# GpSimd makes the last shifted copy of a key tile as one addition of 32-bit integers

## The chip, the cores and the metric

The kernel runs on one core of a Trainium2 chip. The core has TensorE for matrix products (PE, with PEld for loading its weights), VectorE (DVE), ScalarE (ACT), GpSimd (POOL) and SyncE (SP), which issues most transfers. PE writes only to PSUM; the other tiles lie in SBUF. The metric is the device time of one execution in microseconds; less is better. A profile is taken of one execution, and its span is the time from its first to its last instruction.

## The reference

A token matrix x (2048 x 512) goes through two blocks whose results are mixed by a gate for each token:

```python
x = A_x
g = _sigmoid((x * gate_w).sum(-1, keepdims=True))
a = _A_ref(x, A_wqkv, A_wo)                         # attention
b = _B_ref(x, B_w_gate, B_w_up, B_w_down)           # (silu(x @ w_gate) * (x @ w_up)) @ w_down
return g * a + (1 - g) * b

def _A_ref(x, wqkv, wo):
    ...                                             # q, k, v: 32 heads of width 16
    scores = jnp.einsum("bhqd,bhkd->bhqk", q, k) * (Dh ** -0.5)
    p = _softmax(scores, axis=-1)
    o = jnp.einsum("bhqk,bhkd->bhqd", p, v)
    return ... @ wo
```

The attention needs 32 x 2048 x 2048 exponentials. They are the large elementwise work of the kernel.

## The kernel before, in words

**Units and tiles.** The 32 heads are handled in 8 groups of 4, the 2048 queries in 4 blocks of 512. One block of queries with one group of heads is a unit; there are 32. A unit has 16 key tiles of 128 keys. One key tile of a unit is 4 heads x 128 keys x 512 queries: four matmuls of scores, each 128 x 512 in one bank of PSUM, and after the exponential one product with the values ("term") of four small matmuls that run side by side in PE and add into o_ps (function pv, line 972).

**Two ways to the exponential.** Most key tiles go to ACT: PE writes scores to s_t (two tiles of two banks each), ACT turns 128 x 1024 at a time into e_all, PE multiplies it with vaug: one term. Other tiles go to DVE (emit_d, line 845). There PE writes the scores of one head to d_t, in one of three single banks that the feed-forward block uses too (m_tile, line 361), and DVE evicts it with a multiplication and an addition into 16-bit integers, y, whose bits read as bf16 are a rough exponential (line 862). Four evictions of 128 x 512 fill one tile y of 128 x 2048. This rough exponential is bettered in one of two ways:
- *two terms* (groups[n] == 2, lines 869 to 871): DVE takes two parts of y's bits by masks into two more buffers (bits, line 895), multiplies one by y (product, line 904), and PE multiplies both results with the values;
- *four terms* (lines 872 to 876): y itself and three copies of it, each with a constant of SHIFTS (25, 56, 94) added to the 16-bit integers (copy, line 887), so that four rough exponentials with errors at different places are summed by PE.

**Buffers.** y and the copies lie in seven homes of 128 x 2048 16-bit values (NS = 7; six of their own, named c_t, and one that lies in wd_t early on and in kaug's first group later; home, line 836). A home is free when all its users are through: users[i] holds a count and the latest time, and drop (line 823) counts down. y is counted twice for a four-term tile, once for its own term and once for its copies. At most NY = 3 tiles y are alive (y_live).

**The order is written out by a planner.** As the program is built, a plan keeps a clock for PE, DVE and ACT (plan.pe, plan.dve, plan.act), with a price for each instruction, and the functions at the end of the kernel choose at each step which instruction comes next. Engines take their instructions in the order in which they were recorded (ordered, line 156), so the choice is fixed at build time; on the chip only semaphores hold an engine back.
- The main loop (line 1563) issues the scores for ACT at the latest 0.64 us (LATEST) before the plan's ACT runs out of work, and fills PE's time before that with terms whose data the plan holds to be ready (pv_list, line 1403; the list vready has the time from which a term of DVE may be used) and with pieces of the projections and of the feed-forward block.
- fill_dve (line 924) chooses what DVE does next: copies and masks (vops), evictions of d_t (d_wait) or other evictions and elementwise work (owed).
- v_unit (line 1517) says whether another key tile can go to DVE: the last tile of the unit that is worked on, or of the next, if the plan's DVE is through with what it has LEAD (8.0 us, in the last unit LAST, 6.0) before ACT would be through with the unit. v_take then takes the tile away from ACT, and quad (line 1542) says whether it is made with two terms or with four: four where PE had time to spare (spare[0]).

So the counts of tiles on ACT and on DVE, of two-term and four-term tiles, and the order on every engine come out of the plan, and they change when a price in it changes. POOL only clears tiles at the start.

Of the kernel before, what the change touches and what calls it, by code (L numbers as in the profile page):

```python
# [9 lines left out]
ALU = mybir.AluOpType  # L10
AX = mybir.AxisListType
BF16 = mybir.dt.bfloat16
F32 = mybir.dt.float32
U16 = mybir.dt.uint16
F16 = mybir.dt.float16


# [62 lines left out]
def kernel(  # L80
# [12 lines left out]
    nc = tc.nc  # L93
    P = 128
# [10 lines left out]
    QBW = 512  # L105
# [15 lines left out]
    NV = 4  # L121
# [6 lines left out]
    SHIFTS = (25.0, 56.0, 94.0)  # L128
# [12 lines left out]
    const = ctx.enter_context(tc.tile_pool(name="const", bufs=1))  # L141
# [38 lines left out]
            return lambda *a, **kw: ordered(f(*a, **kw))  # L180

    vec = Ordered(nc.vector)
    queue = Ordered(nc.sync)


# [95 lines left out]
    for j in range(4):  # L281
        nc.gpsimd.memset(sel_t[32 * j:32 * j + 1, j:j + 1], 1.0)

    kb = const.tile([P, NB], F32, name="kb")
    gval = const.tile([P, KT], F32, name="gval")
    omg = const.tile([P, KT], F32, name="omg")
# [4 lines left out]


    class Plan:
        pe = dve = act = 0.0
        mode = last = None
        seq = 0
        slot = -1
# [2 lines left out]
    plan = Plan()  # L300
# [10 lines left out]
    FLIP, UNIT_US = 0.105, 0.217  # L311
    TO_ACT, ACT_FIX, ACT_COL, ACT_IN = 0.485, 0.064, 0.4265, 0.167
    ACT_PE, DVE_PE, PE_DVE, ACT_DVE = 0.055, 0.08, 0.24, 0.06

    def spend(mode, mms, ready=0.0):

        plan.seq += 1
        work_at.append((plan.pe, mms))
        plan.pe = max(plan.pe + (FLIP if mode != plan.mode else 0.0), ready) + (0.226 if mode == "F" else UNIT_US) * mms
        plan.mode = mode  # L320
# [40 lines left out]
    def m_tile(name):  # L361
        while m_ready() is None:
            stuck()
        i = min((i for i in range(NM) if banks[i] is not None), key=lambda i: banks[i])
        plan.pe = max(plan.pe, banks[i])
        banks[i] = None
        held[i] = ps_m[i].tile([P, QBW], F32, tag=f"m{i}", name=name)
        return held[i]

    def m_free(ps, t):  # L370
        i = [h is ps for h in held].index(True)
        banks[i], held[i] = t + DVE_PE, None
# [159 lines left out]
    def q_pieces(qb, b):  # L532
# [11 lines left out]
        def end(p, me):  # L544
# [7 lines left out]
            def mag():  # L552
                vec.tensor_scalar(out=aq[:, :].bitcast(U16), in0=qst[:, :].bitcast(U16), scalar1=0x8000, scalar2=None,
                                  op0=ALU.bitwise_or)
                plan.chain = me
                later(0.21, weigh, plan.dve, ("q", b))
# [9 lines left out]
    def q0_pieces(qb):  # L566
# [11 lines left out]
        def clear():  # L578
            vec.tensor_scalar(out=mt[:, 5, :].bitcast(U16), in0=mt[:, 5, :].bitcast(U16), scalar1=0x7FFF, scalar2=None,
                              op0=ALU.bitwise_and)  # L580
# [108 lines left out]
    vops = []  # L689
    c_free = [0.0] * NS  # L690
# [3 lines left out]
    vready = []  # L694
# [4 lines left out]
    def score(ps, b, rows=64):  # L699
        n, j = b // 4, HEADS[b % 4]  # L700
        (qb, g), kt = UNIT[n // KT], n % KT
        r = slice(32 * j // rows * rows, 32 * j // rows * rows + rows)
        q = (q0a if n < KT // 2 else q0[qb])[r, j % 2, :] if g == 0 else get_q(qb, g)[r, j % 2, :]
        mm(ps, lhsT=kaug[r, g, kt * P:(kt + 1) * P], rhs=q, start=True, stop=True,
           tile_position=(r.start, 0))
# [115 lines left out]
    users = {}  # L821

    def drop(i, t):
        u = users[i]
        u[:] = u[0] - 1, max(u[1], t)
        if not u[0]:
            c_free[i] = u[1]

    def take_home():
        i = min(range(NS), key=lambda i: c_free[i])  # L830
        t, c_free[i] = c_free[i], 1e9
        assert t < 1e9
        users[i] = [1, 0.0]
        return i, t

    def home(i=None, t=0.0):

        if i is None:
            i, t = take_home()
        plan.dve = max(plan.dve, t)  # L840
        if i < NS - 1:
            return i, vex.tile([P, NV * QBW], U16, tag=f"h{i}", name="c_t", bufs=1)[:, :]
        return i, (kaug[:, 0, :] if au > QB else wd_t[:, 0:4, :].rearrange("p f d -> p (f d)")).bitcast(U16)

    def emit_d(i, rows=32):
        if not vcur:
            n = v_take()
            waiting[n] = [NV, None, take_home()]
            vcur.update(n=n, left=list(range(NV)), y=None)
            y_live[0] += 1  # L850
        n, left, cur = vcur["n"], vcur["left"], waiting[vcur["n"]]
        left.remove(i)
        d_t = m_tile("d_t")
        score(d_t[:, :], 4 * n + i, rows)
        if not left:
            vcur.clear()

        def first():
            if cur[1] is None:
                cur[1] = home(*cur[2])  # L860
            h, y = cur[1]
            vec.tensor_scalar(out=y[:, i * QBW:(i + 1) * QBW], in0=d_t[:, :], scalar1=EXP_A, scalar2=EXP_B[groups[n]],
                              op0=ALU.mult, op1=ALU.add)
            m_free(d_t, plan.dve)
            cur[0] -= 1
            if cur[0]:
                return
            plan.last = ("y", n)
            if groups[n] == 2:
                vops.extend([(0.6, lambda: bits(n, 0, y), ("y", n), n, True), (0.6, lambda: bits(n, 1, y), None, n, True),  # L870
                             (MUL_US, lambda: product(n, h, y), None, n, False)])
            else:
                users[h][0] = 2
                ready(n, 0, h, y)
                for k in range(1, 4):
                    vops.append((0.6, lambda k=k: copy(n, k, h, y), ("y", n) if k == 1 else None, n, True))
        d_wait.append((plan.pe + UNIT_US + PE_DVE, first, n))

    waiting = {}
    copies = {}  # L880
    part = {}

    def ready(n, k, h, c):
        copies[n, k] = (c.bitcast(BF16), h)
        vready.append((plan.dve + DVE_PE, n, k))

    def copy(n, k, i, y):
        h, c = home()
        vec.tensor_scalar(out=c, in0=y, scalar1=SHIFTS[k - 1], scalar2=None, op0=ALU.add)
        ready(n, k, h, c)  # L890
        if k == 3:
            drop(i, plan.dve + 0.05)
            y_live[0] -= 1

    def bits(n, k, y):
        h, c = home()
        if k == 0:
            vec.tensor_scalar(out=c, in0=y, scalar1=0x007F, scalar2=0x3F00, op0=ALU.bitwise_and, op1=ALU.bitwise_or)
            part[n] = (h, c)
        else:  # L900
            vec.tensor_scalar(out=c, in0=y, scalar1=0xFF80, scalar2=None, op0=ALU.bitwise_and)
            ready(n, 0, h, c)

    def product(n, h, y):
        i, c = part.pop(n)
        vec.tensor_tensor(out=c.bitcast(BF16), in0=y.bitcast(BF16), in1=c.bitcast(BF16), op=ALU.mult)
        ready(n, 1, i, c)
        drop(h, plan.dve + 0.05)
        y_live[0] -= 1
# [411 lines left out]
    for pos, qb in enumerate(ORDER):  # L1321
# [13 lines left out]
        for tq in range(TQ):  # L1335

            def cond(qb=qb):
                return qb == QB - 1 or all((qb, b) in normed for b in range(NB))
            rel = 100 if pos == 0 else (UNIT.index((qb, G - 1)) + 1) * KT + 16
            c = pace.add((out_pieces if pos else down_pieces)(qb, tq), rel, a0 + per * (0.64 + 0.36 * (tq + 1) / TQ),  # L1340
                         (gus if tq == 0 else prev) + gates, cond=cond)
# [10 lines left out]
    au = at_ = quarter = begun = 0  # L1352
    vu = 0
    hi = [KT] * UNITS
# [151 lines left out]

    SLACK = 0.04
    CUTS = 4
    LEAD, LAST = 8.0, 6.0
    TILE_US = 1.82  # L1510

    def forward():
# [4 lines left out]
    def v_unit():  # L1517

        nonlocal vu
        if y_live[0] >= NY or min(c_free) >= 1e9 or sum(v[0] for v in vops) > 4.9 or (au, at_) < (0, 2):  # L1520
            return None
        while vu < UNITS:
            if vu > au + 1 or vu in q_of and not (q_of[vu].done() and (vu < QB or plan.slot >= q_of[vu].done_at + 3)):
                return None
            left = hi[vu] - (at_ + begun if vu == au else 0)
            if vu >= au and left > 0 and (vu or hi[0] > KT // 2):
                end = plan.act + (left - 1) * TILE_US + ((hi[au] - at_) * TILE_US if vu > au else 0.0)
                busy = sum(v[0] for v in vops) + 0.6 * (len(owed) + len(d_wait))
                if plan.dve + busy + (LEAD if vu < UNITS - 1 else LAST) <= end:
                    return vu  # L1530
            vu += 1
        return None

    def v_take():
        un = v_unit()
        hi[un] -= 1
        n = un * KT + hi[un]
        groups[n] = 2 if quad() else 4
        forward()
        return n  # L1540
# [7 lines left out]
    def wants():  # L1548

        if len(d_wait) >= 3 or not vcur and v_unit() is None:  # L1550
            return 0
        return 2 if thirst() < 1.5 else 1
# [10 lines left out]
    while au < UNITS:  # L1563
# [11 lines left out]
        if room > 0.02:  # L1575
# [3 lines left out]
            c = side(room + SLACK)  # L1579
# [30 lines left out]
    while closed < UNITS or vops or vcur:  # L1610
# [9 lines left out]
        c = side(2.0)  # L1620
# [38 lines left out]
    for tq in range(TQ):  # L1659
        t = (QB - 1) * TQ + tq  # L1660
# [39 lines left out]
```

## Time and profile before

| | us |
|---|---|
| time, median of 3 runs | 769.66 (769.5 to 769.75) |
| the profiled execution's own time | 768.54 |
| its span | 766.8 |
| ACT busy in it | 750.8 |
| PE busy | 740.6 |
| DVE busy | 734.6 |
| POOL busy | 10.6 |

The span leaves out what lies around the first and the last instruction: 768.54 - 766.8 = 1.7 us. The granted TensorE clock is 0.999 of full speed. In the rows of the profile, L171 is the helper that records every ACT instruction, L168 that of PE and L180 that of DVE, so groups are told apart by the names of their tiles: e_all<-s_t is an exponential, c_t<-d_t an eviction of scores into y, TENSOR_SCALAR c_t<-c_t of 128x2048 a shifted copy or a mask, TENSOR_TENSOR c_t<-c_t the product of a two-term tile. A row has the count, then the busy time of all and the mean of one in ns, then the idle time of the engine just before them and what ended it. Instructions of one engine overlap a little, so means times counts are more than the busy time.

### The profile page before, as it was taken

What the parts mean: (1) busy time and instruction counts of PE and PEld (TensorE: products, weight loads), DVE (VectorE), ACT (ScalarE), POOL (GpSimd) and SP (SyncE); (2) the same over time, 40 slices, a digit from 0 to 9 for tenths busy, and PEclk for the clock granted to TensorE, in tenths of its full rate; (3) what the DMA queues carried; (4) which work ended last, traced back from release to release, by engine and by line L of the source; (5) the groups of instructions that cost most, each with busy time, mean ns of one, the idle gap of its engine ahead of it and who ended that gap; (6) DMA issues with size and microseconds to landing.
All of it is one profiled execution on the core that took longest, in us unless ns stands there. A gap on an engine that the chain in (4) does not pass through costs nothing.

```text
span 766.8 us, 24169 instructions
## 1 busy us (share of the span) xinstructions
PE 740.6 (97%) x10109; PEld 246.0 (32%) x10109; DVE 734.6 (96%) x1234; ACT 750.8 (98%) x843; POOL 10.6 (1%) x25
## 2 busy tenths in 40 slices
PE   8999999999999999999999999999999999999997
PEld 3333333333333233333333333323333333333332
DVE  7899999999999999999999999999999999999993
ACT  6999999999999999999999999999999999999996
POOL 5000000000000000000000000000000000000000
PEclk9999999999999999999999999999999999999999
DMA  9000313144210013211200130212000232100001
GB/s 222 6 2 15 67 21 78 34 117 87 62 28 13 17 41 78 58 33 28 51 18 24 32 95 21 69 28 56 12 19 17 69 80 56 31 18 7 22 30 35
DMA packets 91029, 34.53 MB, mean 45 GB/s; under 512 B 75488, under 2 KB 90472, under 8 KB 90920
## 3 DMA queue, kind: packets, MB, share of 16 engines
q1 hardware_dynamic: 89192, 32.66, 17.7%
q8 instruction: 79, 1.29, 0.7%
q10 hardware_dynamic: 1728, 0.33, 0.2%
q14 instruction: 30, 0.25, 0.1%
HBM read 21.55 MB, written 2.35 MB: 31 GB/s over the span
## 4 chain that ended last, share of the span: by engine, by line
ACT 48%; PE 27%; DVE 13%; issue 11%; DMA 0%; DVEq 0%; ACTq 0%
ACT e_all L171 45%; DVE c_t L180 9%; PE s_t L168 9%; PE o_ps L168 8%; PE gu L168 5%; ACT th L171 2%; PE dps L168 2%; DVE kaug L180 1%; PE qp L168 1%; DVE mt L180 1%; PE vp L168 1%; PE warm L168 1%; DVE gs L180 1%; DVE osb L180 1%; PE kp L168 0%
## 5 line engine op out<-in xcount | busy, mean ns | idle before, releaser
L171 ACT ACTIVATE e_all<-s_t 128x1024 bf16<-128x1024 f32 x774 | 722.9, 1049 | 3.2 <-PE s_t L168 1.6
L180 DVE TENSOR_SCALAR c_t<-d_t 128x512 uint16<-128x512 f32 x432 | 285.8, 681 | 4.8 <-PE d_t L168 4.5
L168 PE MATMUL s_t<-qx,kaug 32*128 32x512 bf16 (+1 forms) x1224 | 237.6, 385 | 11.6 <-ACT e_all L171 10.2
L168 PE MATMUL o_ps<-e_all,vaug 128*32 128x512 bf16 (+3 forms) x2024 | 170.1, 334 | 0.8 <-ACT e_all L171 0.6
L168 PEld LDWEIGHTS <-kaug 32*128 32x128 bf16 (+1 forms) x2048 | 80.6, 91 | 275.8 <-issue 268.6
L180 DVE TENSOR_SCALAR c_t<-c_t 128x2048 uint16<-128x2048 uint16 x236 | 157.7, 682 | 0.4
L168 PE MATMUL d_t<-qx,kaug 32*128 32x512 bf16 x408 | 153.2, 384 | 0.3 <-DVE qx L180 0.3
L168 PEld LDWEIGHTS <-vaug 128*32 128x32 bf16 x4112 | 101.9, 95 | 131.8 <-issue 94.7
L168 PE MATMUL o_ps<-c_t,vaug 128*32 128x512 bf16 (+3 forms) x1768 | 136.3, 341 | 0.7 <-DVE osb L180 0.6
L168 PE MATMUL gu<-xT,wg 128*32 128x512 bf16 x896 | 71.9, 383 | 0.1
L168 PE MATMUL gu<-xT,wu 128*32 128x512 bf16 x896 | 70.2, 383 | 0.0
L168 PE MATMUL ops<-wd_t,mt 128*32 128x512 bf16 x672 | 58.1, 382 | 0.0
L180 DVE TENSOR_SCALAR kaug<-d_t 128x512 uint16<-128x512 f32 x60 | 40.0, 682 | 0.9 <-PE d_t L168 0.7
L180 DVE SCALAR_TENSOR_TENSOR mt<-gs,gu 128x512 bf16<-128x512 bf16 x56 | 38.1, 680 | 1.6
L180 DVE TENSOR_TENSOR c_t<-c_t 128x2048 bf16<-128x2048 bf16 x32 | 38.8, 1214 | 0.0
L168 PE MATMUL s_t<-q,kaug 32*128 32x512 bf16 (+1 forms) x188 | 36.4, 385 | 2.4 <-ACT e_all L171 2.2
L180 DVE SCALAR_TENSOR_TENSOR gs<-th,gu 128x512 bf16<-128x512 bf16 x56 | 38.0, 678 | 0.1
L171 ACT ACTIVATE th<-gu 128x512 bf16<-128x512 f32 x56 | 35.0, 624 | 0.0
L168 PEld LDWEIGHTS <-mt 128*32 128x32 bf16 (+1 forms) x1037 | 25.0, 95 | 26.2 <-issue 19.6
L180 DVE TENSOR_SCALAR kaug<-c_t 128x2048 uint16<-128x2048 uint16 x46 | 31.3, 680 | 0.0
L180 DVE TENSOR_SCALAR c_t<-kaug 128x2048 uint16<-128x2048 uint16 x42 | 28.1, 683 | 0.0
L168 PEld LDWEIGHTS <-wg 128*32 128x32 bf16 x896 | 18.1, 94 | 25.3 <-issue 21.3
(142 smaller groups left out, 434.1 us busy)
## 6 DMA issues: line engine op xcount, KB each, us to landing
wg<-in_B_w_gate_dram SPq DMA_DIRECT2D x56, 128.0 KB
wu<-in_B_w_up_dram SPq DMA_DIRECT2D x56, 128.0 KB
on<-osb SPq DMA_DIRECT2D x120, 16.0 KB
rb<-rr SPq DMA_DIRECT2D x15, 128.0 KB
wd_t<-in_B_w_down_dram SPq DMA_DIRECT2D x7, 256.0 KB
qx<-qst SPq DMA_DIRECT2D x96, 16.0 KB
qx<-aq SPq DMA_DIRECT2D x96, 16.0 KB
out_dram<-o_t SPq DMA_DIRECT2D x12, 128.0 KB
```

Of the source, the lines that this page charges most:

```text
L168: return ordered(nc.tensor.matmul(*args, **kw))
L171: ordered(nc.scalar.activation(*args, **kw))
L180: return lambda *a, **kw: ordered(f(*a, **kw))
```

## The change

For a four-term tile the third copy (shift 94) is given to POOL when a home is free and POOL's clock in the plan is less than 4 us ahead of DVE's. POOL reads y as 1024 integers of 32 bits for each partition and adds lift, a tile with 94 in both 16-bit halves, broadcast along the row. The addition is recorded when the last eviction of the tile is, so it waits for that eviction and for its home. The plan books 2.5 us for it; y then has three users, and the copies that are left for DVE are two. Where it is not given, DVE makes three copies as before.

```diff
+    gps = Ordered(nc.gpsimd)
...
+    lift = const.tile([P, 2], U16, name="lift")
+    nc.gpsimd.memset(lift[:], int(SHIFTS[2]))
...
-        pe = dve = act = 0.0
+        pe = dve = act = pool = 0.0
...
+    POOL_US, POOL_PE, POOL_AHEAD = 2.5, 0.15, 4.0
...
             else:
-                users[h][0] = 2
+                gives = min(c_free) < 1e9 and plan.pool - plan.dve < POOL_AHEAD
+                users[h][0] = 3 if gives else 2
                 ready(n, 0, h, y)
-                for k in range(1, 4):
-                    vops.append((0.6, lambda k=k: copy(n, k, h, y), ("y", n) if k == 1 else None, n, True))
+                if gives:
+                    a, t = take_home()
+                    c = home(a, 0.0)[1]
+                    gps.tensor_tensor(out=c.bitcast(I32), in0=y.bitcast(I32),
+                                      in1=lift[:, :].bitcast(I32).broadcast_to([P, NV * QBW // 2]), op=ALU.add)
+                    plan.pool = max(plan.pool, plan.dve + 0.1, t) + POOL_US
+                    copies[n, 3] = (c.bitcast(BF16), a)
+                    vready.append((plan.pool + POOL_PE, n, 3))
+                    drop(h, plan.pool + POOL_PE)
+                last = 2 if gives else 3
+                for k in range(1, last + 1):
+                    vops.append((0.6, lambda k=k: copy(n, k, h, y, k == last), ("y", n) if k == 1 else None, n, True))
...
-    def copy(n, k, i, y):
+    def copy(n, k, i, y, last):
...
-        if k == 3:
+        if last:
             drop(i, plan.dve + 0.05)
             y_live[0] -= 1
...
-    LEAD, LAST = 8.0, 6.0
+    LEAD, LAST = 9.0, 7.0
...
-            left = hi[vu] - (at_ + begun if vu == au else 0)
+            left = hi[vu] - (at_ + 1 if vu == au else 0)
```

The last three lines change when a tile may go to DVE: the plan asks for one microsecond more of lead, and the tile that ACT stands at always counts as begun.

More of the change, by code (lines that the diff above doesn't have):

```diff
@@ L14 @@
 U16 = mybir.dt.uint16
+I32 = mybir.dt.int32
 F16 = mybir.dt.float16
```

## The prediction

> **What bounds the kernel now.** I read the page's busy line first, then the busy time by stretches, then what ScalarE (ACT) waits for, then the rows of the instructions that the change touches.
>
> ```profile
> PE 740.6 (97%) x10109; PEld 246.0 (32%) x10109; DVE 734.6 (96%) x1234; ACT 750.8 (98%) x843; POOL 10.6 (1%) x25
> ```
> ```profile
> 20.00:60.00 40.00, 38.62 (x521) 12.71 (x513) 36.42 (x69) 39.16 (x44) 0.00 (x0) 1.00 0.01 4
> 60.00:160.00 100.00, 97.55 (x1341) 31.51 (x1333) 98.69 (x166) 99.80 (x113) 0.00 (x0) 1.00 0.24 52
> 160.00:260.00 100.00, 97.72 (x1375) 32.50 (x1370) 96.64 (x163) 99.37 (x113) 0.00 (x0) 1.00 0.21 49
> 260.00:360.00 100.00, 96.86 (x1351) 33.57 (x1343) 99.47 (x164) 99.72 (x114) 0.00 (x0) 1.00 0.20 47
> 360.00:460.00 100.00, 97.64 (x1336) 31.79 (x1328) 99.05 (x157) 99.89 (x113) 0.00 (x0) 1.00 0.17 43
> 460.00:560.00 100.00, 96.78 (x1353) 32.19 (x1351) 97.61 (x165) 99.80 (x114) 0.00 (x0) 1.00 0.16 37
> 560.00:660.00 100.00, 98.20 (x1366) 32.16 (x1362) 99.25 (x160) 99.80 (x114) 0.00 (x0) 1.00 0.20 49
> 660.00:740.00 80.00, 78.38 (x1078) 24.60 (x1071) 79.76 (x132) 80.00 (x89) 0.00 (x0) 1.00 0.07 20
> ```
> ```profile
> ACT e_all L171 <- PE s_t L168: 1.6, 4, 0.5
> ```
>
> The columns of the stretches are their length, then the busy time of PE, PEld, DVE, ACT and POOL, each with its instructions. From 60 to 740 us ACT is busy over 99% of every stretch, and in the whole run its exponentials wait 1.6 us for scores. ACT sets the end, and DVE stands beside it with almost no reserve: from 20 to 740 us it is busy 706.9 of 720, so 13.1 us idle. POOL does nothing after 12 us.
>
> ```profile
> L171 ACT ACTIVATE e_all<-s_t 128x1024 bf16<-128x1024 f32 x774 | 722.9, 1049 | 3.2 <-PE s_t L168 1.6
> L180 DVE TENSOR_SCALAR c_t<-d_t 128x512 uint16<-128x512 f32 x432 | 285.8, 681 | 4.8 <-PE d_t L168 4.5
> L180 DVE TENSOR_SCALAR c_t<-c_t 128x2048 uint16<-128x2048 uint16 x236 | 157.7, 682 | 0.4
> L180 DVE TENSOR_TENSOR c_t<-c_t 128x2048 bf16<-128x2048 bf16 x32 | 38.8, 1214 | 0.0
> ```
> ```profile
> 309.99 1.88 DVE L180 TENSOR_SCALAR c_t<-d_t 128x512 uint16<-128x512 f32 x3
> ```
> ```profile
> L254 POOL MEMSET kaug<- 128x1024 f32 x3 | 2.7, 957 | 0.0
> ```
>
> An exponential costs ACT 722.9/774 = 0.934 us. DVE instructions overlap a little: three evictions in a row take 1.88 us, so each after the first adds (1.88 - 0.68)/2 = 0.60. A copy counts 0.60 as well, a product 1.14 (1.21 less the same overlap). The copy passes 2048 values in the time in which an eviction passes 512: four times its rate.
>
> **The change, part by part.** What moves was counted in the order of the built instructions; durations are the rows above.
>
> ACT: 774 exponentials become 772, which is 2 x 0.934 = 1.9 us off the bounding engine. One more tile goes to DVE (126 in place of 125). That is all the change takes from ACT: the freed DVE time is hardly turned into more DVE tiles.
>
> DVE: four-term tiles go from 85 to 72, two-term tiles from 40 to 54. Copies and masks fall from 335 to 255 (80 x 0.60 = 48.0 us less), products rise from 40 to 54 (14 x 1.14 = 16.0 more), evictions from 500 to 504 (2.4 more). Sum: 29.6 us less, and DVE's idle time would be 13.1 + 29.6 = 42.7 us. Beside a busy ACT this gains nothing by itself; it is cover for delays.
>
> PE: attention terms fall by 24, and one ACT tile goes: 25 groups of four matmuls at about 0.22 us (12 matmuls of gu, three such groups, take 0.83 us at 299.68, one alone 0.39) is 5.5 us less. Hidden under ACT too: zero. The LEAD, LAST and begun edits only choose which tile goes to DVE when; they are inside these counts. The memset of lift lies in POOL's first 12 us: zero.
>
> POOL: 69 additions of 128x1024, one for all but 3 of the 72 four-term tiles. No row shows such an addition. Nearest is the POOL memset of 1024 32-bit values: 0.957 us, 2.74 for three in a row, so 0.89 a pass, for writing alone. An addition reads the tile, reads lift and writes. One pass, all overlapped, is 0.9 us; three passes, nothing overlapped, 2.7. Two passes would be 1.8. I take 2.25, between two and three; the plan in the code books 2.5. POOL has 69 x 2.25 = 155 us to do in 720, so its load is no bound. By the Trainium skill, "GPSIMD Engine Reference" (3.1 Elementwise), an addition of 2048 fp32 values takes 4497 ns on GpSimd, so 2.25 us would be an estimate for 1024; no run here shows it yet.
>
> **The added wait that decides: the addition against DVE's fast instructions.** Every addition starts when the last eviction of its tile is done, while DVE runs on with its list. What an addition beside a copy costs DVE is shown by no row: the only overlaps are memsets at the start (POOL's q at 5.02 beside DVE's kaug at 4.73: 0.95 and 0.91 us, as long as their like elsewhere), and neither reads SBUF. From below it is 0. From above it is exclusion: copies, masks, products and other instructions of DVE that go from SBUF to SBUF (I call them fast) don't run while an addition runs, nor it while they do; evictions from PSUM do. I take exclusion: a copy has to move four times an eviction's data in the same 0.68 us, so it is likely to hold more ways into SBUF than an eviction, while 69 x 2.25 us of reading and writing by another engine is laid right among the copies of the same tiles.
>
> Then each addition's price follows from DVE's order behind the eviction that releases it. If the next instruction is fast, it goes first, and the addition starts at its end; if not, the addition starts after 0.1 us (what the plan books). With m other instructions of 0.60 us before the next fast one, this waits 2.25 - 0.60m in the first case and 0.1 more in the second.
> - Addition starts at once (27): m is 1 in 18 (wait 1.75), 2 in 3 (1.15), 3 in 1 (0.55), more in 5 (none): 31.5 + 3.5 + 0.6 = 35.5.
> - A fast one goes first (42): m is 1 in 8 (1.65), 2 in 13 (1.05), 3 in 5 (0.45), more in 16 (none): 13.2 + 13.7 + 2.3 = 29.1.
>
> Sum 64.6 us, in 48 waits, mean 1.35. Behind a waiting copy are queued the next evictions of d_t and gu; they give back the three single banks of PSUM, PE waits for one in order, and the next scores stand behind it on PE, so ACT runs dry. What hides part: the plan sends scores at the latest 0.64 us before ACT needs them (LATEST). I let the first 0.64 us of each wait be hidden, and trust that DVE's 42.7 us of idle time makes up for that part before the next addition, some 11 us later: 18 x 1.11 + 3 x 0.51 + 8 x 1.01 + 13 x 0.41 = 34.9 us come through. If all idle time of DVE could be used wherever it lies, 64.6 - 42.7 = 21.9 come through; if nothing is hidden, 64.6. With an addition of 2.7 us the waits sum to 89.0 and 55 come through beyond 0.64; with 0.9 us they sum to 9.6, all below 0.64.
>
> By the Trainium skill, "SBUF — State Buffer" (Who interferes with whom), GpSimd and DVE share one pair of ports; a DVE instruction in a two-port mode, or one with two SBUF inputs against a GpSimd instruction that reads, takes it for its whole length, and the other fully blocks. By this rule the price is the upper one, 64.6 us of waits; were it wrong, 0. The only rows that bear on it, the memsets beside each other, agree with it but don't test it.
>
> A smaller added wait: PE reads the sum where the plan expects it, 2.65 us after the release. An addition behind one copy ends at 0.60 + 2.25 = 2.85: 0.2 us late in at most 42 cases, 8 us at the most. Between the last d_t matmul of a tile and the first that waits for its sum stand 48 to 187 matmuls, 64 in the median, 4.7 us at 73 ns each (740.6/10109). I take nothing for it.
>
> **Sum.** The profiled execution took 768.54 us (span 766.8): 768.5 - 1.9 + 34.9 = 801.5; the median shown, 769.66, is 1.1 above it. **Forecast: 802.7 us**, some 4% slower; by the bounds of hiding 769.66 - 1.9 + 21.9 = 789.7 to 832.4, given exclusion.
>
> **Rivals.**
> - *No exclusion* (the other side). The additions run beside the copies at no cost to DVE; this holds as long as an addition keeps within the plan's 2.65 us. Then the 1.9 us of ACT are gained, and at best its 1.6 us of waits for scores: 769.66 - 1.9 = 767.8, or 766.2. For it: overlapping memsets didn't lengthen each other. Against: no copy was among them. It decides if copies beside an addition keep 0.68 us.
> - *Exclusion, but a short addition.* At 0.9 to 1.2 us the waits sum to 9.6 to 18 us, none above 0.8, and DVE's 42.7 us of idle time cover them: 768 to 771. Against: two inputs and one output at a memset's price.
> - *Long addition without exclusion.* At 3.5 us each, the half of the sums that are read soonest (35) come 0.85 us late, 0.2 of it beyond 0.64: 35 x 0.2 = 7 us, less the 1.9: 775. POOL shows no reason in its rows for more than three passes.
>
> **Chances.** Exclusion with a price that shows: 0.66. No exclusion: 0.20. Short addition: 0.09. Long addition: 0.05. A measurement of this kernel can tell about 0.2% (1.5 us) from no change. Faster by more comes from no exclusion (0.18 of its 0.20) and a little of the short addition (0.02): 0.20. Same: 0.02 + 0.07 = 0.09. Slower: 0.66 + 0.05 = 0.71. The range for 8 in 10 must take in most of the no-exclusion case and the upper bounds of the waits short of the worst: 766 to 835. The likeliest case alone: 787 to 835.
>
> **What would show it.** Right: copies c_t<-c_t with a mean well above 0.68 us, or idle time before them put down to POOL; DVE's evictions unchanged at 0.68; POOL's additions 69 in number, 2 to 3 us each; ACT's waits for s_t grown from 1.6 us to some 30 to 40, spread over all stretches; PE waiting for DVE. Wrong: copies at 0.68 beside running additions, ACT still busy over 99% of the stretches, and a span about 2 us shorter. Wrong in size: if PE waits for c_t sums of POOL itself, or if the waits of DVE vanish in its idle time.

## The result and the profile after

The changed kernel takes 825.1 us (824.97 to 830.06, 4 runs) where the kernel before takes 769.68 beside it: 1.0736 of its time, 95% interval 1.0696 to 1.0776, so 55.4 us slower. The profiled execution took 825.11 us with a span of 823.4.

The page's busy line, and from its groups the rows that answer to those shown of before (count, busy us, mean ns, idle time before):

```profile
PE 759.8 (92%) x10001; PEld 243.3 (30%) x10001; DVE 768.1 (93%) x1172; ACT 759.2 (92%) x841; POOL 159.5 (19%) x95
...
L172 ACT ACTIVATE e_all<-s_t 128x1024 bf16<-128x1024 f32 x772 | 729.6, 1038 | 50.4 <-PE s_t L169 30.0
L181 DVE TENSOR_SCALAR c_t<-d_t 128x512 uint16<-128x512 f32 x444 | 292.0, 680 | 10.1 <-PE d_t L169 9.4
...
L181 POOL TENSOR_TENSOR c_t<-c_t,lift 128x1024 int32<-128x1024 int32 x52 | 111.5, 2144 | 467.7 <-DVE c_t L181 437.2
...
L181 DVE TENSOR_SCALAR c_t<-c_t 128x2048 uint16<-128x2048 uint16 x181 | 149.8, 835 | 4.0 <-PE o_ps L169 2.6
...
L181 DVE TENSOR_TENSOR c_t<-c_t 128x2048 bf16<-128x2048 bf16 x36 | 52.1, 1447 | 0.0
```

Evictions from PSUM kept their 0.68 us. Copies rose from 0.68 to 0.84 in the mean, products from 1.21 to 1.45, and the idle time before exponentials from 3.2 to 50.4 us. No row of DVE names POOL as what it waited for: the lost time stands inside the instructions, as a longer duration. Two stretches of the same busy table as before (length, PE, PEld, DVE, ACT, POOL):

```profile
160.00:260.00 100.00, 93.19 (x1235) 28.69 (x1227) 92.44 (x136) 91.69 (x105) 21.07 (x10) 0.98 0.27 65
...
660.00:760.00 100.00, 90.48 (x1192) 28.31 (x1191) 97.00 (x143) 91.33 (x103) 27.07 (x13) 0.98 0.14 34
```

ACT, over 99% busy before, is at 91 to 92% in the stretches with 10 and 13 additions; their granted clock, 0.98, is taken up in the last section. One case shows the chain from DVE to ACT. These are lines from the timelines of POOL, DVE, PE and ACT of the changed kernel at 411 us (start, length, then what it is; in brackets the idle time before it and what ended it):

```profile
411.04 1.89 POOL L181 TENSOR_TENSOR c_t<-c_t,lift 128x1024 int32<-128x1024 int32 x1 [8.85 <-DVE c_t L181]
```
```profile
411.07 2.42 DVE L181 TENSOR_SCALAR c_t<-c_t 128x2048 uint16<-128x2048 uint16 x1
413.41 1.27 DVE L181 TENSOR_SCALAR kaug<-d_t 128x512 uint16<-128x512 f32 x2
414.61 0.68 DVE L181 TENSOR_SCALAR c_t<-c_t 128x2048 uint16<-128x2048 uint16 x1
```
```profile
413.54 0.40 PE L169 MATMUL o_ps<-c_t,vaug 128*32 128x512 bf16 x4 [1.60 <-DVE c_t L181]
...
414.09 0.39 PE L169 MATMUL s_t<-qx,kaug 32*128 32x512 bf16 x2
```
```profile
414.58 1.02 ACT L172 ACTIVATE e_all<-s_t 128x1024 bf16<-128x1024 f32 x1 [1.41 <-PE d_t L169]
```

The addition starts 0.03 us before a copy. The copy is recorded as 2.42 us long: it ends at 413.49, 0.56 us after the addition's end at 412.93, and alone it lasts 0.68 us, so hardly any of it was done while the addition ran. PE's next instruction is the term that reads this very copy; PE stands for 1.60 us, the scores behind the term start only at 414.09, and ACT stands for 1.41 us. (The profile names a d_t matmul as what ended ACT's wait: it was issued beside the scores and ended last.)

Over the trace, I count as wait what an instruction of DVE that overlaps POOL lasts beyond its like in the kernel before (copies 0.68 us, products 1.21, the small ones from SBUF to SBUF 0.17 to 0.68), where that is over 0.06 us. In the changed kernel these are 53 waits with 58.9 us: copies and masks 39.8, products 9.4, small ones 9.7. The expectations below quote earlier counts of the same kind, 54.9 us for this kernel and 25.9 for the one with planned waits. ACT's side: idle time between its first and last exponential grew from 2.7 to 50.1 us, 47.4; and its busy time by 8.4, although it does two exponentials fewer, because an exponential after a gap costs its full 1.04 us and not the 0.934 that one costs in the mean of before, where most overlap the one ahead of them. With 0.7 us of a later first exponential this is the 56.6 us of span.

### The profile page after: what moved, and what is told of

Its sections match the earlier page's. It is cut to its first block, busy times and chain, and to the rows that moved or that the text cites. A ratio compares the mean times of both kernels' runs of the same rounds, so it can differ in the third digit from the quotient of the medians.

```text
span 823.4 us, 24025 instructions
## 1 busy us (share of the span) xinstructions
PE 759.8 (92%) x10001; PEld 243.3 (30%) x10001; DVE 768.1 (93%) x1172; ACT 759.2 (92%) x841; POOL 159.5 (19%) x95
## 4 chain that ended last, share of the span: by engine, by line
DVE 59%; PE 25%; ACT 9%; issue 6%; DMA 0%; SPq 0%; DVEq 0%; ACTq 0%
DVE c_t L181 39%; ACT e_all L172 8%; PE s_t L169 8%; DVE kaug L181 7%; PE o_ps L169 7%; PE gu L169 4%; DVE mt L181 3%; DVE gs L181 2%; DVE osb L181 2%; DVE on L181 1%; PE d_t L169 1%; PE ops L169 1%; PE qp L169 1%; PE kp L169 1%; DVE qst L181 1%
## 5 line engine op out<-in xcount | busy, mean ns | idle before, releaser
L172 ACT ACTIVATE e_all<-s_t 128x1024 bf16<-128x1024 f32 x772 | 729.6, 1038 | 50.4 <-PE s_t L169 30.0
L181 DVE TENSOR_SCALAR c_t<-d_t 128x512 uint16<-128x512 f32 x444 | 292.0, 680 | 10.1 <-PE d_t L169 9.4
L181 POOL TENSOR_TENSOR c_t<-c_t,lift 128x1024 int32<-128x1024 int32 x52 | 111.5, 2144 | 467.7 <-DVE c_t L181 437.2
L181 DVE TENSOR_SCALAR c_t<-c_t 128x2048 uint16<-128x2048 uint16 x181 | 149.8, 835 | 4.0 <-PE o_ps L169 2.6
L169 PE MATMUL d_t<-qx,kaug 32*128 32x512 bf16 x404 | 146.8, 384 | 7.0 <-DVE c_t L181 3.1
L169 PE MATMUL o_ps<-c_t,vaug 128*32 128x512 bf16 (+3 forms) x1688 | 132.8, 342 | 21.8 <-DVE c_t L181 18.6
L169 PEld LDWEIGHTS <-vaug 128*32 128x32 bf16 x4004 | 99.0, 95 | 163.0 <-issue 130.1
L181 DVE TENSOR_TENSOR c_t<-c_t 128x2048 bf16<-128x2048 bf16 x36 | 52.1, 1447 | 0.0
L181 POOL TENSOR_TENSOR c_t<-kaug,lift 128x1024 int32<-128x1024 int32 x9 | 21.0, 2330 | 101.1 <-DVE kaug L181 101.1
L181 DVE TENSOR_SCALAR kaug<-d_t 128x512 uint16<-128x512 f32 x52 | 34.2, 678 | 1.3 <-PE d_t L169 1.1
```

Source lines behind the costliest of these rows:

```text
L169: return ordered(nc.tensor.matmul(*args, **kw))
L172: ordered(nc.scalar.activation(*args, **kw))
```

## Experiments

The theories: **A**, POOL's addition and DVE's fast instructions exclude one another, and DVE's waits come through in full; **B**, the same, but the first 0.64 us of each wait is hidden, as the prediction had it; **C**, the order or the late sums are the cause.

The first five leave the changed kernel's order as it is or (the fourth) never give POOL a copy.

**Quarter of the addition** (half: 2 in place of 1):

```diff
-gps.tensor_tensor(out=c.bitcast(I32), in0=y.bitcast(I32),
+gave.add((n, 3))
+gps.tensor_tensor(out=c[:, 0:1 * QBW].bitcast(I32), in0=y[:, 0:1 * QBW].bitcast(I32),
...
-e = e_of[b] if k is None else c[:, i * QBW:(i + 1) * QBW]
+at_col = (i % 1 if (n, k) in gave else i) * QBW
+e = e_of[b] if k is None else c[:, at_col:at_col + QBW]
```

> The changed kernel with the same order on every engine, but each POOL addition covers only the first 256 of the 1024 integers; the products of that term read the first 512 columns four times, so three quarters of the third copy are left out and the sums are not the reference's. An addition should last about a quarter of 1.89 us, 0.5 us. Theory A (exclusion, and every wait of DVE comes through in full): no fast DVE instruction waits as long as one eviction of 0.60 us stands before it, so nearly all of the 54.9 us of waits go, and the time falls to about 825.1 - 54.9 = 770. Theory B (exclusion, but the first 0.64 us of each wait is hidden, as the prediction had it): the waits beyond 0.64 us sum to 25.0 in the changed kernel, so the time falls only to about 800, and the rest of the loss is the new order itself. Theory C (no exclusion; the order or the late sums are the cause): DVE's copies stay above 0.8 us or the time stays above 810.

Measured: 773.46 us (772.2 to 774.62), 1.0058 of before (1.0040 to 1.0075). An addition that is not held up lasts 0.61 us; 18 waits, 3.6 us. The copies:

```profile
L181 DVE TENSOR_SCALAR c_t<-c_t 128x2048 uint16<-128x2048 uint16 x181 | 124.3, 694 | 4.0 <-PE o_ps L169 2.7
```

> As the quarter addition, but over 512 of the 1024 integers (half of the third copy is left out; the products read the first two heads' columns twice). An addition should last about 1.0 us. Theory A: counted in the order, the waits sum to 12 us (26 of them, some 0.5 us each), so 770 + 12 = 782. Theory B: no wait is longer than 0.64 us, so the time equals that of the quarter addition within 2 us. Theory C: no step between quarter, half and whole that follows the waits.

Measured, in two runs: 783.35 us, 1.0186 (1.0166 to 1.0207). An addition that is not held up lasts 1.04 us; 31 waits, 16.9 us. The copies:

```profile
L181 DVE TENSOR_SCALAR c_t<-c_t 128x2048 uint16<-128x2048 uint16 x181 | 130.5, 728 | 4.0 <-PE o_ps L169 2.7
```

A did better than B and C. With the same order on every engine, 51.6 us lie between whole and quarter, so the new order alone can't be the cause (B left it some 30 us, at 800), and the half addition, which B had within 2 us of the quarter, stands 9.9 us above it. But "in full" is too much: 13.3 us more waits cost these 9.9 us.

**POOL only writes:**

```diff
-gps.tensor_tensor(out=c.bitcast(I32), in0=y.bitcast(I32),
-                  in1=lift[:, :].bitcast(I32).broadcast_to([P, NV * QBW // 2]), op=ALU.add)
+gps.memset(c.bitcast(F32), 0.0)
```

> The changed kernel with the same order on every engine, but POOL clears the home (a memset of 128x1024 32-bit values, which reads nothing) in place of the addition, so the third copy is left out and counts as zero. The memset should last 0.96 us as at the start of the kernel. If an instruction of POOL that only writes excludes DVE's fast instructions too, the copies wait as with the half addition: some 11 us in about 26 waits, and about 781 by theory A. If exclusion needs POOL to read, or holds only for DVE's products (two inputs), the copies keep 0.68 us and the time is that of the quarter addition, about 770.

Measured, in two runs: 777.99 us, 1.0117 (1.0097 to 1.0137), with 24 waits, 11.1 us. Its rows of copies and products:

```profile
L181 DVE TENSOR_SCALAR c_t<-c_t 128x2048 uint16<-128x2048 uint16 x181 | 127.8, 714 | 3.5 <-PE o_ps L169 2.4
...
L181 DVE TENSOR_TENSOR c_t<-c_t 128x2048 bf16<-128x2048 bf16 x36 | 43.7, 1214 | 0.0
L181 DVE TENSOR_SCALAR kaug<-c_t 128x2048 uint16<-128x2048 uint16 x37 | 25.6, 692 | 0.3
```

Both answers at once: copies wait for an instruction that only writes, products don't. All 54 products are at 1.21 us, the 8 that overlapped a clearing among them, and 3 of these began while it was running. Of the 12 that overlapped a whole addition, 8 began while it was running, and all 8 waited; the other 4 had begun before it. The Trainium skill, "SBUF — State Buffer" (Who interferes with whom), makes the same difference: a DVE instruction with two SBUF inputs contends with a GpSimd instruction that reads, not with one that only writes. The runs agree.

**The rest of the change without POOL:**

```diff
-gives = min(c_free) < 1e9 and plan.pool - plan.dve < POOL_AHEAD
+gives = False
```

> The changed kernel where POOL is never given a copy, so that of the change only the later points at which tiles go to DVE are left (LEAD 9, LAST 7, the begun tile). All theories: no addition, copies at 0.68 us. ACT does some 774 exponentials again, so 768 to 773 us; above 775 the edits of LEAD, LAST and begun would be a cause of their own.

Measured: 771.48 us, 1.0033 (1.0020 to 1.0045), with 776 exponentials: two more than before, which is 1.9 of the 2.7 us. The LEAD, LAST and begun edits are a small loss of their own in this order.

**Four pieces:**

```diff
-gps.tensor_tensor(out=c.bitcast(I32), in0=y.bitcast(I32), ...
+for q in range(4):
+    qs = slice(q * NV * QBW // 4, (q + 1) * NV * QBW // 4)
+    gps.tensor_tensor(out=c[:, qs].bitcast(I32), in0=y[:, qs].bitcast(I32), ...
```

> The changed kernel with the same order on every engine, but each addition is made as four additions of 256 integers, one behind the other on POOL; all of the copy is computed. By the quarter and half additions a piece lasts 0.61 us alone (0.19 fixed and 1.66 ns an integer), so the four last some 2.0 to 2.5 us. If exclusion holds for the length of one instruction, a fast DVE instruction gets its turn between two pieces and waits 0.6 us at the most: about 48 waits of 0.3 us mean, some 15 to 20 us, and the time is near 785 to 790. If POOL keeps DVE out as long as it has work queued, the waits grow with the longer sum (52.6 us counted for 2.0 us, over 70 for 2.4) and the time is 825 to 845.

Measured, in two runs: 787.81 us, 1.0241 (1.0220 to 1.0261). 67 waits, 22.1 us, the longest 0.45. So exclusion lasts for one instruction: between two pieces DVE gets its turn, although POOL is busier (213 us with additions in place of 149) in the same order. This run also decides against B: none of its waits goes beyond 0.64 us, yet it is 14.3 us above the quarter addition, with 18.5 us more waits. And it rules out late sums, the other half of C: a tile's sum is done 4.2 us (median) after its first piece begins, 2.2 in the changed kernel, and still the time is 37 us less and no wait of PE for POOL stands in its list.

**A planner that knows of the exclusion:**

```diff
-POOL_US, POOL_PE, POOL_AHEAD = 2.5, 0.15, 4.0
+POOL_US, POOL_PE, POOL_AHEAD = 1.95, 0.15, 4.0
...
+def shut(now):
+    return plan.p0 - 0.1 < now < plan.p1 - 0.05
...
 def pay_v():
+    if shut(plan.dve):
+        plan.dve = plan.p1
...
-fit = bool(vops) and vops[0][3] // KT <= closed + AHEAD and c_ready() <= now
+fit = bool(vops) and vops[0][3] // KT <= closed + AHEAD and c_ready() <= now and not shut(now)
```

> The changed kernel with a planner that knows of the exclusion: it books 1.95 us for an addition, holds DVE's copies, masks and products back until the plan's addition ends, and gives DVE evictions meanwhile (LEAD 8, LAST 6). 73 additions, 772 exponentials as in the changed kernel. Counted in its order the waits are 28 us in 47 places, most of them now in the plan. Theory A (the loss is exclusion that the plan did not know, and a wait that is planned for does not hold PE or ACT up): 768 to 773 us. If the loss belongs to POOL's work as such, planned or not, the 28 us of waits come through and it is about 798.

Measured: 787.11 us, 1.0231 (1.0215 to 1.0246): a miss for the number of A. 35 waits with 27.1 us were left, which the plan did not know: 12.1 before small instructions (the products on<-on,rb and their like, small copies), 15.1 before copies and products. My reading of the latter: the plan lets a copy go at the very moment at which the addition is released, so the addition starts late and ends up to 0.5 us later than booked.

> As the kernel with planned waits, but with LEAD 9 and LAST 7 and four tiles y alive (NY 4 in place of 3): 76 additions, 770 exponentials, 17 us of waits counted in the order in 52 places, 16 of them over 0.64 us. Theory A: four exponentials fewer than before are 3.7 us, so 765 to 770, the first version that could be level with the kernel before or a little faster. If the loss belongs to POOL's work as such: 771 + 17 = 788.

Measured: 776.64 us, 1.0094 (1.0077 to 1.0111), with 21 waits, 16.4 us. This is above the range that was given for A, so a miss too, and 10.5 us below the other. Holding back the small instructions too, and moving the plan's addition behind the copy that goes first:

```diff
+late = plan.dve + vops[0][0] - plan.p0
+if plan.dve < plan.p0 and late > 0:
+    plan.p0, plan.p1, plan.pool = plan.p0 + late, plan.p1 + late, plan.pool + late
...
-due = [k for k, o in enumerate(owed) if o[0] <= now + 0.05]
+due = [k for k, o in enumerate(owed) if o[0] <= now + 0.05 and not (o[1] in (0.345, 0.21, 0.4) and shut(now))]
```

> The kernel with planned waits (LEAD 8, LAST 6, three tiles y alive), where the plan now also holds back the smaller instructions of DVE from SBUF to SBUF (the products on<-on,rb, the magnitudes aq) while an addition runs, and shifts an addition by the copy that the plan lets go first. 74 additions, 772 exponentials. In the kernel with planned waits the plan still missed 25.9 us of waits, 10.8 of them before these smaller instructions. Theory A (only waits that the plan does not know cost time): the missed waits should fall to some 10 us, and with 0.6 to 0.8 of each coming through the time is 775 to 779, well under 787. If the missed waits were not the cause of the 787, it stays within 784 to 790.

Measured: 774.84 us, 1.0074 (1.0059 to 1.0089), with 14 waits, 13.8 us. Against planned_waits with the same LEAD and LAST this is 12.3 us less for 13.3 us less of waits. The page's row of its exponentials, for comparison with the changed kernel's:

```profile
L172 ACT ACTIVATE e_all<-s_t 128x1024 bf16<-128x1024 f32 x772 | 722.2, 1049 | 8.3 <-PE s_t L169 5.2
```

The same 772 exponentials, beside 74 whole additions, with 8.3 us of idle time in place of 50.4: POOL's work as such does not cost the 55 us.

> The same planner with LEAD 9, LAST 7 and four tiles y alive: 68 additions, 774 exponentials, as many as in the kernel before. Theory A: missed waits as small as in its sister, so 771 to 777; it cannot be faster than before by more than 0.2%, since ACT has all its exponentials again. If it is under 767, freed DVE time is worth something on its own and the bound is read wrongly.

Measured: 774.78 us, 1.0076 (1.0059 to 1.0092), with 11 waits, 7.9 us. It is 5.5 us above before with equally many exponentials. Its waits are enough to explain that if most of them come through, but whether they do, or other delays are in it, was not settled.

All runs on one line, by DVE's waits:

| kernel | waits: number, us | longest us | time us |
|---|---|---|---|
| before | 0 | - | 768.8 to 769.7 |
| the rest of the change without POOL | 0 | - | 771.5 |
| quarter addition | 18, 3.6 | 0.4 | 773.5 |
| planned, small ones too, NY 4 | 11, 7.9 | 1.7 | 774.8 |
| only writes | 24, 11.1 | 0.8 | 778.0 |
| planned, small ones too | 14, 13.8 | 1.7 | 774.8 |
| planned, NY 4 | 21, 16.4 | 1.7 | 776.6 |
| half addition | 31, 16.9 | 0.9 | 783.4 |
| four pieces | 67, 22.1 | 0.45 | 787.8 |
| planned | 35, 27.1 | 1.7 | 787.1 |
| changed kernel | 53, 58.9 | 1.7 | 825.1 |

In the five kernels with the changed kernel's order, a microsecond of wait more than the quarter addition has costs 0.61 us (only writes: 4.5 for 7.5), 0.75 (half), 0.78 (four pieces) and 0.93 (whole: 51.6 for 55.3). The last holds some microseconds of a lower TensorE clock (last section). No version with POOL beat the kernel before.

## Why the prediction was right, and where its sizes were off

The direction and the mechanism were right; 802.7 was forecast, 825.1 measured. One size was off by much (5), and another error hid part of that (3).

1. *ACT sets the end, DVE has no reserve.* Right. The waits of DVE turned into idle time of ACT in all runs.
2. *ACT gains 1.9 us.* The count was right (772), but it is seen in no time: the quarter addition has the 772 exponentials and 3.6 us of waits, and it is 4.7 us above before. The rival without exclusion, at 767.8 or less, was too low for this order as well, as far as the quarter addition shows it.
3. *The addition takes 2.25 us.* It takes 1.89 when it is not held up (31 of 69 lie between 1.89 and 1.90), 2.2 to 3.1 when a copy or a product goes first, for then its recorded length has the wait in it. By the figure of the Trainium skill, "GPSIMD Engine Reference" (3.1 Elementwise), which is for fp32, it would be 2.25 as an estimate; the measurement decides, 16% less. From quarter, half and whole (0.61, 1.04, 1.89 us) it is 0.18 us fixed and 1.67 ns an integer. The overlong addition was luck for the total: with 2.0 us the prediction's own rule lets 24.4 us come through and gives 792, so 10 us of the miss in 5 were hidden by it.
4. *Exclusion, 64.6 us of waits in 48 places.* Right: 58.9 us in 53. With 2.0 us for the addition (1.89 and its start) the same count of the order gives 52.6 in 48; the row-by-row count of what follows each releasing eviction was good to some 12%. With the rule of the Trainium skill, "SBUF — State Buffer" (Who interferes with whom), the runs agree in each part that they test: copies wait for a POOL instruction that reads and writes and for one that only writes, products only for one that reads, each for the length of one instruction.
5. *The first 0.64 us of each wait is hidden, DVE's idle time makes up for it; 34.9 of 64.6 come through.* This is the term that was mis-sized. Beyond 0.64 us lie only 27.3 of the 58.9 us, yet 51.6 us more than in the quarter addition came through. Waits of at most 0.45 us (four pieces) came through at 0.78. DVE still had 35 us of idle time from 20 to 797 us by the busy table, but it lies where the static order makes DVE wait for others (9.4 us for d_t, 7.6 for one output), not behind the additions. The bound with nothing hidden (832.4, with the addition at 2.25 us) was nearer.
6. *The path: evictions late, banks late, PE waits for a bank.* Half right. Three of PE's waits in the changed kernel, none of which stands in the list of the kernel before:

```profile
PE o_ps L169 <- DVE c_t L181: 18.6, 22, 1.7
...
PE d_t L169 <- DVE c_t L181: 4.0, 9, 0.9
...
PE gu L169 <- DVE c_t L181: 2.7, 4, 1.5
```

   Most often it is the term that reads the late copy itself, put by the plan right behind the copy's expected end (22 times, 18.6 us, up to 1.7); banks come after it (d_t and gu). This is the likely reason why so little is hidden: between the copy and its reader the plan leaves 0.08 us (DVE_PE), and LATEST does not apply to that path. No run moved the reader away from its copy, so this part is argued and not shown.
7. *Sums late by themselves: nothing.* Right. No wait of PE for POOL stands in the list of the changed kernel, and the later sums of the four pieces cost nothing that can be seen.

## What to carry to other kernels

Before work goes to GpSimd beside a busy VectorE, look at what VectorE does in the microseconds after: here its copies from SBUF to SBUF stood still until the GpSimd addition was through, its evictions from PSUM didn't, and the profile shows this only as longer copies. Where the order is fixed at build time, count most of each such wait, however short (0.6 to 0.9 came through here); slack elsewhere did not make up for it. Price the gain on the engine that sets the end first: here 69 copies, some 41 us of VectorE's work, were moved for two exponentials of 774, and even with the waits planned for (774.8) nothing was won.

## What the runs showed of the hardware

All 36 copies and masks that waited for an addition ended 0.55 us after it, all 8 products 1.08, though they last 0.68 and 1.21 alone: they go on as soon as the addition is through, without further loss. POOL's addition, in turn, waits for a copy that is under way; released 0.16 us after the start of one, it was recorded 0.38 us longer (300.70, with 2.27 us). All 37 additions that were recorded at over 2 us began while a copy, mask or product of 128x2048 was under way, and none of the other 32 did. The evictions of scores that overlapped an addition kept 0.62 to 0.69 us.

The granted TensorE clock, 1.00 in all stretches of before from 20 to 740 us, was 0.98 in three stretches of the changed kernel. Each holds one piece of 3.4 us at half the clock, from 224.4, 326.8 and 753.5 us; PE is busy throughout these pieces, and ACT is idle for 3.4 of their 10.2 us. At half speed PE does 5.1 us less work in them, so by estimate 3 to 5 of the 55.4 us are the clock's. PE had stood for 0.8 to 2.9 us shortly before each piece, but waits as long elsewhere in the same run (1.69 us up to 303.6) were not followed by one, so what sets such a piece off is not shown. The kernel with planned waits has three such pieces as well, the one with the small instructions held back none.
